# Weights cast by their transfers, attention inputs cast two tiles ahead, and first feed-forward groups of two tiles

## The chip, the core and the metric

The kernel runs on one core of a Trainium2 chip. The metric is the device time of one execution in microseconds (us). The engines are TensorE (PE; its weight loads are listed as PEld), VectorE (DVE), ScalarE (ACT), GpSimd (POOL) and SyncE (SP, which here only issues transfers). Each works through its own instructions in order and waits for the others by semaphores.

## What is computed

Block-wise linear attention with a decay per head, and then a feed-forward layer on the normalized result. Inputs and output are float32; batch 4, 8 heads, 768 positions, head width 64, model width 512, hidden width 2048.

```
# per head: lam; blocks of positions; state kv starts at 0 for each batch
intra = (q_b @ k_b.T) * (lam ** (i - j) for i >= j, else 0) @ v_b
inter = (q_b * lam ** (pos + 1)) @ kv
x     = intra + inter                                  # [batch, seq, 512]
kv    = lam ** block * kv + (k_b * lam ** (block - 1 - pos)).T @ v_b
xn    = (x - mean(x)) / sqrt(var(x) + 1e-6) * g_ln
out   = x + relu(xn @ w_ch1) @ w_ch2
```

## The kernel before

A tile is 128 positions of one batch with all heads and all 512 columns: 24 tiles, six per batch, t from 0 to 23, c = t mod 6 its place in the batch. Attention is done tile by tile with the block length 128. The decay of the mask is split: values are multiplied by lam to a negative power (lam_v), what comes out of the attention by lam to a positive power (lam_q), and the mask is a plain triangle (tril).

The work of a tile has five steps. p0 issues the loads of a later tile and casts q and k to bf16 and v times lam_v to bf16, all three on POOL (bf_inputs). p1 transposes k and q on PE (tk, tq) and copies them out of PSUM (kTp on ACT in two halves, qT on DVE). p2 computes the scores sc, masks them into mA on DVE, and, but for the last tile of a batch, the update pk of the state: for c = 0 Sn is written by DVE, otherwise DVE adds the old state (Stmp) and POOL multiplies by the block's decay (Sn). p3 computes po from mA and from the state of the tile before, scales it on DVE to x, and does the LayerNorm: stats, mv, xc (x minus its mean, bf16) on DVE, std on ACT, rstd on DVE. The scale g_ln is not in xc but multiplied into the rows of w_ch1; rstd comes last of all, in the output. p4 transposes xc (xt) and copies it to xT on ACT.

The feed-forward layer takes tiles in groups: [0..3], [4, 5], then four at a time, and the last [22, 23]. m1 is one of 16 units of a group, four matmuls with up to 512 columns into one PSUM buffer and a relu to hT on ACT. m2 is one of four parts of a tile, four matmuls; behind the last part DVE computes o = rstd times the sum, plus x, and SP stores it.

The order is written out by hand: nothing reorders it. The list `steps` holds the attention steps of tile after tile, shifted by one (p1 of tile j, p3 of j-1, p2 of j, p0 of j+1, p4 of j-1). The steps up to p4 of tile 3 run first. Then the steps of the next group's tiles are spread evenly between the units of a group. Weights come as float32 into six staging buffers by SP's queue and are cast by DVE, ACT and POOL in pieces between the units of the first group, w_ch1 times g_ln.

PSUM has two "aux" buffers, which tk, tq, pk and xt take in turn, so that of four allocations per round each waits for the reader of the last but one: a tk takes the buffer that pk had in the round before. There are three "mm" buffers for m1 and m2. k, q and v of a tile each have six input buffers.

Of the kernel before, what the change touches and what calls it, by code (L numbers as in the profile page):

```python
# [16 lines left out]
def kernel(  # L17
# [56 lines left out]
    def load_w1(c):  # L74
        f = wst.tile([128, KA, W1C], F32, tag="wst", name="w1f")
        nc.sync.dma_start(f, moe_w_ch1[:, c * W1C:(c + 1) * W1C].rearrange("(k p) f -> p k f", p=128))
        w_stage["w1", c] = f

    def load_w2(c):
        f = wst.tile([128, W2K, DM], F32, tag="wst", name="w2f")  # L80
        nc.sync.dma_start(f, moe_w_ch2[c * W2K * 128:(c + 1) * W2K * 128, :].rearrange("(k p) d -> p k d", p=128))
        w_stage["w2", c] = f

    def cast_w1(c):
        f = w_stage.pop(("w1", c))
        for kk in range(KA):
            dst = w1[:, kk, c * W1C:(c + 1) * W1C]
            if kk % 2 == 0:
                nc.vector.tensor_scalar_mul(dst, f[:, kk, :], g_col[:, kk:kk + 1])
            elif kk == 1:  # L90
                nc.scalar.mul(dst, f[:, kk, :], g_col[:, kk:kk + 1])
            else:
                nc.gpsimd.tensor_scalar_mul(dst, f[:, kk, :], g_col[:, kk:kk + 1])  # L93

    def cast_w2(c):
        f = w_stage.pop(("w2", c))
        for i in range(W2K):
            dst = w2[:, c * W2K + i, :]
            if i % 2 == 0:
                nc.vector.tensor_copy(dst, f[:, i, :])  # L100
            elif i == 1:
                nc.scalar.copy(dst, f[:, i, :])
            else:
                nc.gpsimd.tensor_copy(dst, f[:, i, :])
# [3 lines left out]
    load_tile(0)  # L108
    g_col = const.tile([128, KA], F32)
    nc.sync.dma_start(g_col, moe_g_ln.rearrange("(k p) -> p k", p=128))  # L110
    load_tile(1)
    load_tile(2)
    load_tile(3)
    load_w1(0)
    load_w1(1)
    load_tile(4)
    load_w1(2)
    load_w1(3)
    for c in range(NWC):
        load_w2(c)  # L120
    load_tile(5)
# [141 lines left out]
    def mlp_units(g):  # L263
        hT = gp.tile([128, KB, GT * 128], BF16, tag="hT", bufs=1, name="hT")
# [32 lines left out]
        for n in range(KB):  # L297
            yield "m1", n, lambda n=n: m1(n)

        lead = min(3, n_t) if g == 0 else 1  # L300
        order = [(i, part) for part in range(KB // 4) for i in range(lead)]
        order += [(i, part) for i in range(lead, n_t) for part in range(KB // 4)]
        for i, part in order:
            yield "m2", part, lambda i=i, part=part: m2(i, part)
# [13 lines left out]
    steps = [(p0, 0)]
    for j in range(NT + 1):
        lone = j - 1 == groups[0][-1]  # L320
        if j < NT and not lone:
# [71 lines left out]
```

## Time and profile before

| | |
|---|---|
| median of 3 runs | 271.66 us (270.94 to 271.92) |
| the profiled execution's own time | 271.69 us |
| its span, first to last instruction | 270.0 us |
| PE busy | 221.7 us (82%) |
| PEld busy | 128.6 us (48%) |
| DVE busy | 132.7 us (49%) |
| ACT busy | 113.2 us (42%) |
| POOL busy | 82.8 us (31%) |
| moved by DMA | 33.83 MB, mean 125 GB/s |

All times in the rows are counted from the start of the span. Busy times are sums over instructions; a matmul's length has its way through the array in it, so that a lone one is longer than one in a row of many. In brackets or behind a bar stands how long the engine was idle ahead of an instruction, and what released it.

### The profile page before, as it was taken

The numbers are of one execution on the slowest core, as the hardware profiler recorded it, in microseconds if no ns is written. First come the engines' busy times: TensorE is split into PE (matmuls) and PEld (weight loads), VectorE is DVE, ScalarE is ACT, GpSimd is POOL, SyncE is SP. The second block draws the span as 40 slices with busy tenths as digits, with TensorE's granted clock in tenths as the row PEclk, the third lists the DMA queues.
The fourth block names the chain that finished last, engine by engine and source line by source line (L and its number), as shares of the span: only waits on it lengthen the run. The fifth ranks groups of instructions, "written<-read, shape, count | busy, mean of one in ns | idle before, by whom it ended". The sixth has DMA issues, their size and how long they took to land. (4 is left out here: it accounts for less than half of the span.)

```text
span 270.0 us, 4247 instructions
## 1 busy us (share of the span) xinstructions
PE 221.7 (82%) x1638; PEld 128.6 (48%) x1664; DVE 132.7 (49%) x261; ACT 113.2 (42%) x223; POOL 82.8 (31%) x105
## 2 busy tenths in 40 slices
PE   0445448977995766999989999999999899999994
PEld 0334323533554563455545544555555454544761
DVE  2474492728466633754556525664555370335101
ACT  0542225844315523267521575225663217620540
POOL 1414557286002345370052254700513531000000
PEclk9999999999999979999999999999999999999999
DMA  6999964999989650594080971162000211001202
GB/s 129 206 268 304 379 232 164 270 194 225 218 212 240 121 117 0 125 211 93 2 191 8 255 143 31 44 153 79 0 2 0 78 41 39 0 30 50 78 2 78
DMA packets 83395, 33.83 MB, mean 125 GB/s; under 512 B 76080, under 2 KB 76336, under 8 KB 83376
## 3 DMA queue, kind: packets, MB, share of 16 engines
q1 hardware_dynamic: 79216, 32.52, 50.7%
q10 hardware_dynamic: 4160, 1.05, 2.2%
q8 instruction: 13, 0.21, 0.4%
q14 instruction: 6, 0.05, 0.1%
HBM read 27.27 MB, written 6.29 MB: 124 GB/s over the span
## 5 line engine op out<-in xcount | busy, mean ns | idle before, releaser
L271 PE MATMUL pm<-xT,w 128*128 128x512 bf16 (+1 forms) x435 | 93.8, 356 | 2.8 <-POOL w L93 1.1
L282 PE MATMUL pm<-w,hT 128*128 128x512 bf16 x371 | 88.6, 379 | 2.3 <-DVE w L100 1.6
L273 ACT ACTIVATE hT<-pm 128x512 bf16<-128x512 f32 (+1 forms) x112 | 58.3, 534 | 26.1 <-PE pm L271 24.3
L221 POOL TENSOR_TENSOR Sn<-Stmp,lamC 128x512 bf16<-128x512 f32 x16 | 20.4, 1277 | 130.4 <-DVE Stmp L220 130.4
L271 PEld LDWEIGHTS <-w 128*128 128x128 bf16 x448 | 42.8, 100 | 36.4 <-issue 3.0
L282 PEld LDWEIGHTS <-hT 128*128 128x128 bf16 x384 | 35.9, 98 | 38.3 <-DVE w L100 2.1
L193 DVE COPY qT<-tq 128x512 bf16<-128x512 bf16 x24 | 10.2, 424 | 58.8 <-PE tq L191 58.8
L185 PE MATMUL tk<-ident,kb 128*128 128x128 bf16 x96 | 10.3, 235 | 30.0 <-POOL kb L176 30.0
L293 DVE SCALAR_TENSOR_TENSOR o<-pm,rstd,x 128x512 f32<-128x512 f32 (+1 forms) x25 | 17.9, 724 | 32.8 <-PE pm L282 32.8
L206 DVE TENSOR_TENSOR mA<-sc,tril 128x512 bf16<-128x512 f32 x48 | 30.6, 678 | 3.8 <-PE sc L204 3.8
L236 DVE TENSOR_TENSOR x<-po,lam_q 128x512 f32<-128x512 f32 x24 | 16.6, 692 | 28.4 <-PE po L233 26.8
L260 ACT COPY xT<-xt 128x512 bf16<-128x512 bf16 x24 | 14.0, 585 | 35.9 <-PE xt L259 35.9
L245 ACT ACTIVATE std<-mv,eps_t 128x1 f32<-128x1 f32 x24 | 7.1, 295 | 47.2 <-DVE mv L241 47.2
L178 POOL TENSOR_TENSOR vb<-vin,lam_v 128x512 bf16<-128x512 f32 x24 | 25.5, 1063 | 3.4 <-DMA vin<-in_v_dram 1.8
L187 ACT COPY kTp<-tk 64x512 bf16<-64x512 bf16 x24 | 13.8, 575 | 30.2 <-PE tk L185 30.1
L185 PEld LDWEIGHTS <-kb 128*128 128x128 bf16 x96 | 6.6, 103 | 37.7 <-POOL kb L176 35.8
L204 PE MATMUL sc<-qT,kTp 128*128 128x128 bf16 x192 | 17.0, 237 | 2.5 <-DVE qT L193 2.4
L204 PEld LDWEIGHTS <-kTp 128*128 128x128 bf16 x192 | 14.2, 107 | 7.5 <-ACT kTp L188 1.7
L239 DVE BATCH_NORM_STATS2 stats<-x 128x6 f32<-128x512 f32 x24 | 16.7, 695 | 0.8
L174 POOL CAST qb<-qin 128x512 bf16<-128x512 f32 x24 | 15.0, 625 | 6.2 <-DMA qin<-in_q_dram 6.2
L176 POOL CAST kb<-kin 128x512 bf16<-128x512 f32 x24 | 14.9, 620 | 0.0
L259 PE MATMUL xt<-ident,xc 128*128 128x128 bf16 x96 | 10.2, 234 | 5.2 <-DVE xc L243 5.1
(44 smaller groups left out, 156.9 us busy)
## 6 DMA issues: line engine op xcount, KB each, us to landing
qin<-in_q_dram SPq DMA_DIRECT2D x24, 256.0 KB, 4.7
vin<-in_v_dram SPq DMA_DIRECT2D x24, 256.0 KB, 5.0
out_dram<-o SPq DMA_DIRECT2D x23, 256.0 KB, 2.2
kin<-in_k_dram SPq DMA_DIRECT2D x20, 256.0 KB, 4.9
w1f<-in_moe_w_ch_dram SPq DMA_DIRECT2D x4, 1024.0 KB, 7.4
w2f<-in_moe_w_ch_dram SPq DMA_DIRECT2D x4, 1024.0 KB, 8.5
kin<-in_k_dram ACTq DMA_DIRECT2D x4, 256.0 KB, 7.1
out_dram<-o SPq DMA_DIRECT2D x2, 128.0 KB, 1.7
```

Source lines behind the costliest of these rows:

```text
L174: nc.gpsimd.tensor_copy(qb, qf)
L178: nc.gpsimd.tensor_tensor(vb, vf, lam_v[:, :, None].to_broadcast([128, H, D]), op=ALU.mult)
L185: nc.tensor.transpose(tk[:, p, :], s["kb"][:, 2 * p:2 * p + 2, :], ident)
L204: nc.tensor.matmul(sc[:, i, :], lhsT=s["kT"][:, h // 2, h % 2, :], rhs=s["qT"][:, h // 2, :], start=(i == 0), stop=(i == H // 2 - 1), skip ...
L206: nc.vector.tensor_tensor(mA[:, half * (H // 2):(half + 1) * (H // 2), :], sc, tril[:, None, :].to_broadcast([128, H // 2, 128]), op=ALU.mult)
L221: nc.gpsimd.tensor_tensor(Sn, tmp, lamC, op=ALU.mult)
L236: nc.vector.tensor_tensor(x.rearrange("p (h d) -> p h d", h=H), po, lam_q[:, :, None].to_broadcast([128, H, D]), op=ALU.mult)
L239: nc.vector.bn_stats(stats, x)
L271: nc.tensor.matmul(pm[:, 0:N], lhsT=w1[:, kk, n * 128:(n + 1) * 128], rhs=xT_of[g][:, kk, 0:N], start=(kk == 0), stop=(kk == KA - 1))
L273: nc.scalar.activation(hT[:, n, 0:N], pm[:, 0:N], ACT.Relu)
L282: nc.tensor.matmul(acc[i], lhsT=hT[:, kk, i * 128:(i + 1) * 128], rhs=w2[:, kk, :], start=(kk == 0), stop=(kk == KB - 1))
L293: nc.vector.scalar_tensor_tensor(o[:, sl], in0=a[:, sl], scalar=rstd, in1=x[:, sl], op0=ALU.mult, op1=ALU.add)
```

## The change

The weights are loaded by POOL's queue with a cast on the way, straight into four bf16 tiles for w_ch1 and four for w_ch2; staging buffers and cast instructions are gone. g_ln is spread over all partitions (g_row) by one transfer on ACT's queue and multiplied in xc, which becomes a scalar_tensor_tensor. lam_q is multiplied in the cast of q, so that x is a plain copy out of PSUM, now on ACT. bf_inputs casts k first. The loads of k, q, v all go by SP's queue, k first; two memsets of one column on POOL hold the loads of tiles 4 and 5 back until POOL has come to that place. kb and vb have four buffers, xT three, hT two. The groups are [0, 1], [2, 3], [4, 5] and the rest as before; p0 of tile j+2 stands in round j; the order up to tile 5 is written out.

```diff
@@ load_tile @@
-        for name, src in (("q", q), ("k", k), ("v", v)):
+        for name, src in (("k", k), ("q", q), ("v", v)):
             f = inp.tile([128, H, D], F32, tag=name + "in", name=name + "in")
-            eng = nc.scalar if name == "k" and t < 4 else nc.sync
-            eng.dma_start(f, src[b, :, c * C:(c + 1) * C, :].rearrange("h p d -> p h d"))
-            got.append(f)
+            if after_pool:
+
+                nc.gpsimd.memset(f[:, 0, 0:1], 0.0)
+                after_pool = False
+            nc.sync.dma_start(f, src[b, :, c * C:(c + 1) * C, :].rearrange("h p d -> p h d"))
+            got[name] = f
...
     def load_w1(c):
-        f = wst.tile([128, KA, W1C], F32, tag="wst", name="w1f")
-        nc.sync.dma_start(f, moe_w_ch1[:, c * W1C:(c + 1) * W1C].rearrange("(k p) f -> p k f", p=128))
-        w_stage["w1", c] = f
+        nc.gpsimd.dma_start(w1[c], moe_w_ch1[:, c * W1C:(c + 1) * W1C].rearrange("(k p) f -> p k f", p=128))
...
-    g_col = const.tile([128, KA], F32)
-    nc.sync.dma_start(g_col, moe_g_ln.rearrange("(k p) -> p k", p=128))
...
+    g_row = const.tile([128, DM], F32)
+    nc.scalar.dma_start(g_row, moe_g_ln[None, :].to_broadcast([128, DM]))
...
+        kb = wk.tile([128, H, D], BF16, tag="kb", bufs=4, name="kb")
+        nc.gpsimd.tensor_copy(kb, f["k"])
         qb = wk.tile([128, H, D], BF16, tag="qb", name="qb")
-        nc.gpsimd.tensor_copy(qb, qf)
...
+        nc.gpsimd.tensor_tensor(qb, f["q"], lam_q[:, :, None].to_broadcast([128, H, D]), op=ALU.mult)
...
-        nc.vector.tensor_tensor(x.rearrange("p (h d) -> p h d", h=H), po,
-                                lam_q[:, :, None].to_broadcast([128, H, D]), op=ALU.mult)
+        nc.scalar.copy(x, po.rearrange("p h d -> p (h d)"))
...
-        nc.vector.tensor_scalar(xc, x, mv[:, 0:1], None, op0=ALU.subtract)
+        nc.vector.scalar_tensor_tensor(xc, in0=x, scalar=mv[:, 0:1], in1=g_row, op0=ALU.subtract, op1=ALU.mult)
...
-    groups = [[0, 1, 2, 3], [4, 5]]
+    groups = [[0, 1], [2, 3], [4, 5]]
...
+    def round_of(j):
+        steps = []
+        if j < NT:
+            steps.append((p1, j))
+        if j > 0:
+            steps.append((p3, j - 1))
+        if 0 < j and j + 2 < NT:
+            steps.append((p0, j + 2))
+        if j < NT:
+            steps.append((p2, j))
+        if j > 0:
+            steps.append((p4, j - 1))
+        return steps
...
+    p0(0)
+    p0(1)
+    run((p1, 0), (p2, 0))
+    bf_inputs(2)
+    load_w1(0)
+    load_w1(1)
+    run((p1, 1), (p3, 0), (p2, 1), (p4, 0))
+    bf_inputs(3)
+    load_w1(2)
+    load_w1(3)
+    run((p1, 2), (p3, 1), (p2, 2), (p4, 1))
+    load_tile(4, after_pool=True)
+    run((p1, 3), (p3, 2), (p2, 3))
+    for c in range(NWC):
+        load_w2(c)
+    load_tile(5, after_pool=True)
+    load_tile(6)
+    load_tile(7)
+    m1a, m2a = mlp(0)
+    m1b, m2b = mlp(1)
...
+    m1s(m1a, 0)
+    run((p4, 2), (p3, 3))
+    m1s(m1a, 1)
+    p4(3)
+    m1s(m1a, 2)
+    p0(4)
+    for c in range(3):
+        m1s(m1b, c)
+    m1s(m1a, 3)
+    p1(4)
+    m1s(m1b, 3)
+    order = [(m2a, i, part) for part in range(KB // 4) for i in range(2)]
+    order += [(m2b, i, part) for i in range(2) for part in range(KB // 4)]
+    extra = {0: [(p2, 4)], 2: [(p0, 5)], 3: [(p3, 4)], 6: [(p4, 4)], 7: [(p1, 5)], 8: [(p0, 6)], 10: [(p2, 5)], 12: [(p3, 5)], 13: [(p0, 7)], 15: [(p4, 5)]}
```

Three pieces show how instructions move. The first is POOL's order in the head of the kernel before, from the v cast of tile 1 to the state of tile 2.

```order
L178 TENSOR_TENSOR vb<-vin,lam_v 128x512
L221 TENSOR_TENSOR Sn<-Stmp,lamC 128x512
L174 CAST qb<-qin 128x512
L176 CAST kb<-kin 128x512
L178 TENSOR_TENSOR vb<-vin,lam_v 128x512
L221 TENSOR_TENSOR Sn<-Stmp,lamC 128x512
```

The casts of tile 2 stand behind the state of tile 1. Now the same place after the change, from the v cast of tile 2 on; w_0 to w_3 are the four tiles of w_ch1, kin is the input buffer of tile 4.

```order
L142 TENSOR_TENSOR vb<-vin,lam_v 128x512
L75 DMA w_0_75<-in_moe_w_ch_dram 128x4x512
L75 DMA w_1_76<-in_moe_w_ch_dram 128x4x512
L185 TENSOR_TENSOR Sn<-Stmp,lamC 128x512
L138 CAST kb<-kin 128x512
L140 TENSOR_TENSOR qb<-qin,lam_q 128x512
L142 TENSOR_TENSOR vb<-vin,lam_v 128x512
L75 DMA w_2_77<-in_moe_w_ch_dram 128x4x512
L75 DMA w_3_78<-in_moe_w_ch_dram 128x4x512
L185 TENSOR_TENSOR Sn<-Stmp,lamC 128x512
L63 MEMSET kin 128x1
L185 TENSOR_TENSOR Sn<-Stmp,lamC 128x512
```

The casts of tile 2 stand ahead of the state of tile 1, those of tile 3 ahead of the state of tile 2, and four weight transfers stand between them. The last pair is one round on DVE, first before the change.

```order
L193 COPY qT<-tq 128x512
L236 TENSOR_TENSOR x<-po,lam_q 128x512
L239 BN_STATS stats<-x 128x6
L241 BN_AGGR mv<-stats 128x2
L243 TENSOR_SCALAR xc<-x,mv 128x512
L247 RECIPROCAL rstd<-std 128x1
L206 TENSOR_TENSOR mA<-sc,tril 128x512 x2
L220 TENSOR_TENSOR Stmp<-pk,Sn 128x512
```

And after it:

```order
L157 COPY qT<-tq 128x512
L202 BN_STATS stats<-x 128x6
L204 BN_AGGR mv<-stats 128x2
L206 SCALAR_TENSOR_TENSOR xc<-x,mv,g_row 128x512
L210 RECIPROCAL rstd<-std 128x1
L170 TENSOR_TENSOR mA<-sc,tril 128x512 x2
L184 TENSOR_TENSOR Stmp<-pk,Sn 128x512
```

x has left the engine and xc has a second input; the LayerNorm of the tile before still stands ahead of the mask and of Stmp.

## Rows read from the trace of the kernel before

**Rows 1.** Busy us (and instructions) of each engine by stretch; then PEclk, DMA share, GB/s.

```profile
0.00:41.20 41.20, 16.23 (x141) 12.49 (x141) 22.18 (x47) 13.20 (x24) 16.57 (x26) 1.00 0.99 249
41.20:79.50 38.30, 33.99 (x211) 17.12 (x215) 20.55 (x38) 18.21 (x34) 16.85 (x20) 1.00 1.01 217
79.50:112.60 33.10, 23.62 (x236) 17.24 (x237) 18.76 (x38) 12.89 (x32) 10.37 (x13) 0.95 0.54 117
112.60:252.10 139.50, 133.94 (x960) 72.59 (x978) 68.78 (x135) 62.75 (x118) 39.00 (x48) 1.00 0.32 76
```

**Rows 2.** Timeline, tile 2's round: start, length, engine, line, operation [idle before, releaser].

```profile
22.53 0.61 PE L185 MATMUL tk<-ident,kb 128*128 128x128 bf16 x4 [3.70 <-POOL kb L176]
...
23.61 0.42 DVE L193 COPY qT<-tq 128x512 bf16<-128x512 bf16 x1 [3.58 <-PE tq L191]
...
23.84 0.58 ACT L188 COPY kTp<-tk 64x512 bf16<-64x512 bf16 x1
...
24.46 0.69 DVE L236 TENSOR_TENSOR x<-po,lam_q 128x512 f32<-128x512 f32 x1 [0.43 <-PE po L233]
...
25.20 0.64 PE L213 MATMUL pk<-vb,kb 128*128 128x128 bf16 x4
...
26.13 0.49 DVE L243 TENSOR_SCALAR xc<-x,mv 128x512 bf16<-128x512 f32 x1
...
27.79 0.68 DVE L220 TENSOR_TENSOR Stmp<-pk,Sn 128x512 f32<-128x512 f32 x1
...
28.55 1.26 POOL L221 TENSOR_TENSOR Sn<-Stmp,lamC 128x512 bf16<-128x512 f32 x1 [5.07 <-DVE Stmp L220]
...
30.31 0.61 POOL L176 CAST kb<-kin 128x512 bf16<-128x512 f32 x1
...
30.98 0.61 PE L185 MATMUL tk<-ident,kb 128*128 128x128 bf16 x4 [3.70 <-POOL kb L176]
```

**Rows 3.** PE's waits from 112.6 us to its end: total us, times, longest.

```profile
PE tk L185 <- POOL kb L176: 4.6, 7, 1.2
```

**Rows 4.** Timeline of the start: POOL and SP's queue.

```profile
2.31 2.85 SPq L110 DMA_DIRECT2D g_col<-in_moe_g_ln_dram  x1
...
6.93 0.61 POOL L174 CAST qb<-qin 128x512 bf16<-128x512 f32 x1 [4.98 <-DMA qin<-in_q_dram]
...
9.58 1.04 POOL L178 TENSOR_TENSOR vb<-vin,lam_v 128x512 bf16<-128x512 f32 x1 [1.48 <-ACT lam_v L155]
...
15.10 1.72 SPq L76 DMA_DIRECT2D w1f<-in_moe_w_ch_dram  x2
```

**Rows 5.** Groups by form: total busy us, mean ns, idle before them and releasers.

```profile
L273 ACT ACTIVATE hT<-pm 128x512 bf16<-128x512 f32 x80 | 46.6, 594 | 21.9 <-PE pm L271 20.9 <-PE pk L213 0.3
...
L178 POOL TENSOR_TENSOR vb<-vin,lam_v 128x512 bf16<-128x512 f32 x24 | 25.5, 1063 | 3.4 <-DMA vin<-in_v_dram 1.8 <-ACT lam_v L155 1.5
...
L293 DVE SCALAR_TENSOR_TENSOR o<-pm,rstd,x 128x512 f32<-128x512 f32 x23 | 17.0, 745 | 30.1 <-PE pm L282 30.1
...
L273 ACT ACTIVATE hT<-pm 128x256 bf16<-128x256 f32 x32 | 11.7, 383 | 4.2 <-PE pm L271 3.5
```

**Rows 6.** Chain that ended last, three of its PE pieces: start, length, piece.

```profile
216.90 0.45 PE sc L204 x8
...
217.57 2.59 PE pm L282 x12
...
252.10 7.12 PE pm L271 x64
```

**Rows 7.** Timeline, PE, the first long run of m1 matmuls.

```profile
41.76 5.96 PE L271 MATMUL pm<-xT,w 128*128 128x512 bf16 x18 [0.44 <-DVE w L89]
```

**Rows 8.** The page's GB/s of 40 equal slices of 6.75 us.

```profile
GB/s 129 206 268 304 379 232 164 270 194 225 218 212 240 121 117 0 125 211 93 2 191 8 255 143 31 44 153 79 0 2 0 78 41 39 0 30 50 78 2 78
```

**Rows 9.** The page's DMA issues: KB each, median us from issue to landing.

```profile
w1f<-in_moe_w_ch_dram SPq DMA_DIRECT2D x4, 1024.0 KB, 7.4
```

**Rows 10.** Timeline, DVE, the xc of tile 4.

```profile
60.72 0.97 DVE L243 TENSOR_SCALAR xc<-x,mv 128x512 bf16<-128x512 f32 x1
```

More of the change, by code (lines that the diff above doesn't have):

```diff
@@ L39 @@
     GT = 4
-    NG = NT // GT
     NWC = 4
@@ L74, in load_w1 @@
     def load_w1(c):
[L75 to L77 removed]
+        nc.gpsimd.dma_start(w1[c], moe_w_ch1[:, c * W1C:(c + 1) * W1C].rearrange("(k p) f -> p k f", p=128))
     def load_w2(c):
[L80 to L104, printed above, removed]
+        nc.gpsimd.dma_start(w2[c], moe_w_ch2[c * W2K * 128:(c + 1) * W2K * 128, :].rearrange("(k p) d -> p k d", p=128))
     lam_b = const.tile([128, H], F32)
     nc.sync.dma_start(lam_b, lam[None, :].to_broadcast([128, H]))
[L108 to L121 removed]
+    for t in range(4):
+        load_tile(t)
+    g_row = const.tile([128, DM], F32)
+    nc.scalar.dma_start(g_row, moe_g_ln[None, :].to_broadcast([128, DM]))
     ident = const.tile([128, 128], BF16)
@@ L295, in m2 @@
                     nc.sync.dma_start(out[b, c * C:(c + 1) * C, sl], o[:, sl])
[L297 to L304, printed above, removed]
-    groups = [[0, 1, 2, 3], [4, 5]]
+        return m1, m2
+    groups = [[0, 1], [2, 3], [4, 5]]
     while groups[-1][-1] < NT - 1:
@@ L312, in p0 @@
     def p0(t):
-        if t + 5 < NT and t > 0:
-            load_tile(t + 5)
+        if t > 3 and t + 4 < NT:
+            load_tile(t + 4)
         bf_inputs(t)
[L318 to L321, printed above, removed]
+    def round_of(j):
+        steps = []
+        if j < NT:
             steps.append((p1, j))
@@ L324, with run, m1s @@
             steps.append((p3, j - 1))
-        if j < NT and not lone:
+        if 0 < j and j + 2 < NT:
+            steps.append((p0, j + 2))
+        if j < NT:
             steps.append((p2, j))
-            if j + 1 < NT and j != groups[0][-1]:
-                steps.append((p0, j + 1))
         if j > 0:
             steps.append((p4, j - 1))
-        if lone:
-            steps += [(p0, j), (p1, j), (p2, j), (p0, j + 1)]
+        return steps
+    def run(*steps):
+        for f, *a in steps:
+            f(*a)
+    p0(0)
[18 more added lines that the diff above has]
+    m1b, m2b = mlp(1)
+    def m1s(f, c):
+        for n in range(c * W2K, (c + 1) * W2K):
+            f(n)
+    m1s(m1a, 0)
[12 more added lines that the diff above has]
+    extra = {0: [(p2, 4)], 2: [(p0, 5)], 3: [(p3, 4)], 6: [(p4, 4)], 7: [(p1, 5)], 8: [(p0, 6)], 10: [(p2, 5)], 12: [(p3, 5)], 13: [(p0, 7)], 15: [(p4, 5)]}
+    for u, (f, *a) in enumerate(order):
+        f(*a)
+        run(*extra.get(u, []))
+    steps = []
+    for j in range(6, NT + 1):
+        steps += [s for s in round_of(j) if s not in ((p3, 5), (p4, 5))]
     def upto(g):
@@ L337 @@
     pos = 0
-    def run_steps(end):
-        nonlocal pos
-        while pos < end:
-            f, t = steps[pos]
-            f(t)
-            pos += 1
-    run_steps(upto(0))
-    cast_w1(0)
-    w1_cast, w2_cast = 1, 0
-    for g in range(len(groups)):
-        units = list(mlp_units(g))
+    for g in range(2, len(groups)):
+        m1, m2 = mlp(g)
+        units = [(m1, n) for n in range(KB)]
+        units += [(m2, i, part) for i in range(len(groups[g])) for part in range(KB // 4)]
         first, end = pos, upto(g + 1)
         span = len(units) - 2
-        for u, (kind, n, unit) in enumerate(units):
-            if g == 0:
-                if kind == "m1" and n % 4 == 2 and w1_cast < NWC:
-                    cast_w1(w1_cast)
-                    w1_cast += 1
-                if (kind == "m1" and n == KB - 1) or (kind == "m2" and w2_cast < NWC and n >= w2_cast - 1):
-                    cast_w2(w2_cast)
-                    w2_cast += 1
-            unit()
-            run_steps(min(end, first + ((end - first) * (u + 1)) // span))
+        for u, (f, *a) in enumerate(units):
+            f(*a)
+            stop = min(end, first + ((end - first) * (u + 1)) // span)
+            run(*steps[pos:stop])
+            pos = stop
 _INS = ['q', 'k', 'v', 'lam', 'moe_g_ln', 'moe_w_ch1', 'moe_w_ch2']
```

28 lines of the change are left out of this document (12 added, 16 removed).

## The prediction

> **What bounds the kernel now.** I read the table of stretches first [rows 1]. Its columns show that TensorE (PE) is busy 16.2 of the first 41.2 us, 34.0 of the next 38.3 (the feed-forward part of tiles 0 to 3), 23.6 of the 33.1 after that (tiles 4 and 5), and 133.9 of 139.5 from 112.6 us on. So the late part is at its limit and all that can be won in bulk lies ahead of 112.6 us. What limits the head is in the timeline of one round, tile 2 [rows 2]: the first transposes tk start at 22.53, the last DVE instruction of the round, Stmp, ends at 28.47 (5.94 us later), POOL then needs Sn (1.26), qb and kb, and the next tk starts at 30.98. It waited 3.70 us for kb. The loop of 8.45 us per tile is therefore tk, copies, LayerNorm and mask on DVE, then three POOL instructions. From 112.6 us on the same wait for kb is still there seven times, 4.6 us in all [rows 3].
>
> The sum is made against the profiled execution: span 270.0, its time 271.69, so 1.7 lie around the span; the median of the runs is 271.66, the same to 0.03.
>
> **Part by part.** *Casts two tiles ahead.* kb(j) no longer stands behind Sn(j-1). What is late next is a PSUM buffer: tk, tq, pk and xt share two "aux" buffers, so tk(j+1) takes the one of pk(j) and waits until Stmp(j) has read it. The round becomes tk to Stmp: 5.94 us plus the edits on that path. x moves from DVE to ACT; there it follows the second kTp copy, which ends at 24.42, where DVE started it at 24.46 [rows 2]. A PSUM copy there costs 0.58 to 0.60 (the kTp row, the 512-wide hT row [rows 2, 5]) against 0.69, so -0.1. xc becomes a scalar_tensor_tensor, which takes 0.745 as o against 0.49 [rows 2, 5]: +0.25. Round: 6.1 us in place of 8.45. qb rises from a cast to a multiplication with a broadcast, 1.06 like vb [rows 5]; POOL then has about 0.6 + 1.06 + 1.06 + 1.26 = 4.0 us per tile, under 6.1, and no one waits for it as long as it runs ahead. Sn(j) is wanted only by Stmp(j+1) and by po in the round after.
>
> *The start.* g_col with its 2.85 us on SP's queue goes, g_row takes one 256 KB transfer on ACT's queue, and the four k loads leave that queue, behind which ACT made its tables: vb waited for lam_v until 9.58 [rows 4]. k is now the first load; q landed at 6.93 before. I put kb(0) at 5, qb(0) (needs lam_q, too) and vb(0) done at 8.8, Sn(0) at 11.4, Stmp(1) at 16.9 (tq(1) waits for pk(0)'s buffer, then about 5.5), Stmp(2) at 23.0. The first m1 matmul stands behind pk(3) in PE's order; pk ends 3.3 us into a round [rows 2]: 26.4 us, against 41.2. **Term A: -14.8.**
>
> *Weights by casting transfers on POOL's queue.* The 32 weight casts on DVE, ACT and POOL go. Two prices are not in the trace. How long POOL is held per transfer: SP needed 0.86 each for the same pieces, and 2.85 for g_col's 512 single values [rows 4]; I take 1.2, near the first. POOL issues w1_0 and w1_1 after vb(2), at 14.6, before Sn(1). At up to 2.5 us each nothing waits (Sn(1) done by 20.9, wanted by Stmp(2) near 22.4). At 2.85 each the delays pass through Sn(1), vb(3), Sn(2) and Sn(3) and cost about 4. How fast they land: a w1f piece took 7.4 us with another in flight [rows 9], the kernel moved 304 and 379 GB/s where weights dominated and 129 to 206 in the first two slices [rows 8]. At 304: w1_0 lands by 23, before 26.4. w2 is issued after Sn(3), about 31, with tiles 5 to 7 beside it, 6.5 MB in 21.5 us: the last chunk at 52.5 against a need near 51.5. I take +1. At 206 GB/s from 15.6 on the 8.4 MB take 41 us (+5), at 379 nothing waits.
>
> *The first two groups.* PE has 14.2 us of m1 (2 x 7.12), 64 x 0.216 = 13.8 of m2, and attention: a tile is 0.45 for the eight matmuls of sc, so 0.22 for the four each of tk, tq, pk and xt, and about 0.45 for po, 1.78; here tiles 4 and 5 and three remaining pieces, 4.2 [rows 6]. Sum 32.3. The first matmuls of the old stretch ran 18 in 5.96 us where 18 x 0.216 = 3.9 [rows 7]; I keep that loss of 2. ACT's 256-wide hT takes 0.383 of the 0.445 of a unit [rows 5, 6]; the 3.2 us of other copies in that stretch find only 2.0 of room: +1.2. With +1 for w2, 36.5: the stretch ends at 62.9. Before it took 38.3. **Term B: -1.8.**
>
> *The stretch of tiles 4 and 5.* Its matmuls are 14.0 plus attention of four and a half tiles, 8.3, so 22.3; but m1 units of 0.44 are too short to cover rounds of 6.1. 0.4 to the first tk, 4.0 for tile 6 (no state, no LayerNorm ahead of its mask, only the wait of tq(7) for pk(6)), three rounds of 6.1, and 6.1 us of matmuls behind tk(10): 28.8 against 33.1. **Term C: -4.3.**
>
> *From there on* work and order of PE are the same; its rounds of 8.7 us cover 6.1, so the 4.6 us of waits go [rows 3]. Bounds: 0 to -4.6. **Term D: -4.6.**
>
> *xc against POOL.* The old xc was seen at 0.97 where POOL was at work, against 0.49 [rows 2, 10]. xc now reads two tensors from SBUF while POOL's casts run at any time. Between nothing and one vb (1.06) in each of the seven rounds that bound (three in A, four in C), 0 to 7.4; I take **+3**, nearer to the first since POOL works 4.0 of 6.1 us and only part of an instruction is left when met. The Trainium skill ("SBUF — State Buffer", "Summary: rules for kernel authors") says that a VectorE instruction with two SBUF inputs and a GpSimd one that reads SBUF fully block each other, the second to issue waiting. By that rule in the worst phase the sum is 4.4 higher; the 0.97 agrees with the blocking, and does not tell how often it strikes.
>
> Span: 270.0 - 14.8 - 1.8 - 4.3 - 4.6 + 3 = 247.5; with 1.7 around it **249 us**, -8%.
>
> **Rivals.** *Weights come late.* Casting may move less than plain loads do; every us by which the last w2 chunk passes 51.5 is lost, since m2 of the first group needs it and what follows is at its limit. For: nothing in the trace casts on the way; the first slices show 129 and 206 GB/s. Against: pieces of 2 KB moved at 304 and more [rows 8]. At 206: 255; at 165, 51 us, the last chunk at 67: 264. The Trainium skill ("DMA: Bandwidth & Descriptors", section Bandwidth) has 6.15 us for 1 MB issued from GpSimd, without a cast; eight end to end would land at about 65, by which the sum is 262. No row here shows such a transfer.
>
> *Slower than before.* The same mechanism, further: the gain of 22.7 is used up when the last chunk lands at 51.5 + 22.7 = 74, that is below 8.4 MB / 58 us = 144 GB/s. At the slowest rate of the page, 129, it lands at 81: 278 us. For: that slice exists, with 256-byte pieces. Against: the weights' own slices are more than twice as fast.
>
> *POOL held by issuing.* Above 2.5 us each, at 2.85 to 4, 253 to 262. For: POOL writes them beside its casts; against: 0.86 on SP.
>
> *The round stays long.* If casts, not Stmp, still release tk (loads late, POOL behind), rounds stay at 8.45: A loses 4.7, C its 4.3, D its 4.6: 263.
>
> *The gain of D is larger or the chain shorter* (ACT frees x sooner, no xc collision): 244 to 246.
>
> **Chances.** Forecast with the small variations around it (243 to 255) 0.60, weights late 0.15, POOL held 0.09, long round 0.08, slower 0.07, something that cancels to no change 0.01. The range takes in late weights and a long round up to 265: 243 to 265. No change means within 0.5%, 1.4 us, about what this kernel's measurement can tell: faster 0.91, same 0.02, slower 0.07.
>
> **What would show it.** First m1 matmul near 26 us (A), with tk waiting for DVE's Stmp, not for POOL, and head rounds near 6.1. A w2 wait of about 1 us at m2 near 50 (B); more than 5 is the first rival. Two-tile stretch of tiles 4 and 5 near 29 us with tk waits of 1 to 2 us (C). No tk wait on kb after it (D). POOL's gap at its four w1 issues: under 2.5 each. xc's mean between 0.75 and 1.0. The forecast is wrong if m1 starts later than 32 us, if PE waits for a weight chunk more than 5 us in all, or if rounds are 8 us again.

## The result, and the profile after

The changed kernel takes **246.41 us** (246.32 to 246.46, four runs) where the kernel before took 271.79 in the same session (270.94 to 272.61): ratio 0.9066, 95% interval 0.9038 to 0.9094. The forecast was 249. The profiled execution has a span of 244.7 us and took 246.38, so 1.7 lie around the span, as before. Of the span, 25.3 us went (270.0 - 244.7).

The table of stretches of the changed kernel answers to [rows 1], cut at the places that correspond: the first m1, the start of the stretch of tiles 4 and 5, its end, and the place 17.9 us ahead of the end of the span (252.1 before). Columns: stretch, its length, busy us (and instructions) of PE, PEld, DVE, ACT, POOL, then granted clock, DMA share, GB/s.

```profile
0.00:27.50 27.50, 13.13 (x120) 11.20 (x121) 13.42 (x30) 12.79 (x22) 17.84 (x28) 1.00 1.07 183
27.50:62.90 35.40, 33.42 (x283) 23.18 (x281) 15.06 (x29) 18.41 (x47) 19.37 (x22) 1.00 1.13 204
62.90:93.10 30.20, 23.83 (x257) 17.42 (x257) 21.25 (x38) 16.82 (x39) 14.37 (x17) 1.00 1.09 226
93.10:226.80 133.70, 133.70 (x980) 73.23 (x979) 63.67 (x122) 68.69 (x132) 40.47 (x42) 1.00 0.32 75
226.80:244.70 17.90, 13.92 (x96) 9.06 (x93) 2.31 (x4) 6.13 (x16) 0.00 (x0) 0.96 0.12 44
```

| stretch | before, us | after, us | difference | forecast |
|---|---|---|---|---|
| head, to the first m1 (A) | 41.2 | 27.5 | -13.7 | -14.8 |
| feed-forward of tiles 0 to 3 (B) | 38.3 | 35.4 | -2.9 | -1.8 |
| tiles 4 and 5 (C) | 33.1 | 30.2 | -2.9 | -4.3 |
| the rest (D) | 157.4 | 151.6 | -5.8 | -4.6 |
| xc against POOL | | in A to C | | +3 |
| span | 270.0 | 244.7 | -25.3 | -22.5 |

Before, the first matmul of m1 starts at 40.74, 0.46 us ahead of the cut at 41.2; counted from it, A is -13.2 and B -3.4.

Read the fourth line of the fence: PE is busy for all of its 133.70 us. Before, the same work had 133.94 busy in 139.50 [rows 1]. By this measure the late part has reached its limit, and PE's waits lie in the first three stretches. The table of PE's waits of the changed kernel (for what, total us, times, longest) shows which:

```profile
PE tk L149 <- POOL kb L138: 6.7, 1, 6.7
PE xt L222 <- DVE xc L206: 4.9, 8, 1.2
PE tq L155 <- ACT kTp L152: 2.6, 2, 1.3
PE tk L149 <- ACT xT L223: 1.8, 4, 0.7
...
PE tq L155 <- DVE Stmp L184: 1.2, 3, 0.4
PE pm L234 <- DVE o L256: 1.1, 1, 1.1
```

The one wait of tk for kb is the very first transpose of the kernel, which waits for its input; the waits for POOL in the rounds and behind 112.6 us [rows 2, 3] are gone. No wait for a weight stands in the table. What holds the rounds now is LayerNorm (xc) and ACT's copies (kTp, xT).

The timeline of the changed kernel answers to [rows 2]: tile 2's round, from tk to the next tk.

```profile
17.38 0.59 PE L149 MATMUL tk<-ident,kb 128*128 128x128 bf16 x4 [0.67 <-ACT xT L223]
...
18.66 0.58 ACT L152 COPY kTp<-tk 64x512 bf16<-64x512 bf16 x1
...
19.30 0.59 PE L155 MATMUL tq<-ident,qb 128*128 128x128 bf16 x4 [1.33 <-ACT kTp L152]
...
20.77 0.58 ACT L200 COPY x<-po 128x512 f32<-128x512 f32 x1 [1.53 <-PE po L197]
...
22.34 0.75 DVE L206 SCALAR_TENSOR_TENSOR xc<-x,mv,g_row 128x512 bf16<-128x512 f32 x1
...
24.26 0.68 DVE L184 TENSOR_TENSOR Stmp<-pk,Sn 128x512 f32<-128x512 f32 x1
24.43 0.59 PE L149 MATMUL tk<-ident,kb 128*128 128x128 bf16 x4 [0.67 <-ACT xT L223]
```

tk starts again after 7.05 us (8.45 before). It was let go by ACT's copy xT, not by Stmp: at 24.43 Stmp has only begun. And tq waits 1.33 us until both kTp copies of its own tile have read tk: tq has to take tk's buffer.

The transfers of the weights. First POOL's issues in the timeline, then the page's lines for their landing (median, by bytes written) and their queue, beside [rows 4, 9]:

```profile
16.89 1.68 POOL L75 DMA_DIRECT2D w<-in_moe_w_ch_dram  x2
...
22.35 1.55 POOL L75 DMA_DIRECT2D w<-in_moe_w_ch_dram  x2
...
31.93 3.03 POOL L78 DMA_DIRECT2D w<-in_moe_w_ch_dram  x4
```

```profile
q0 software_dynamic: 4224, 4.19, 10.8%
...
w<-in_moe_w_ch_dram POOLq DMA_DIRECT2D x8, 512.0 KB, 7.8
```

POOL is held 0.76 to 0.84 us by each (the mean of a row), as SP was. The queue's packets take 10.8% of 16 engines over the span, 26.4 us of all engines, for 8.39 MB read in fp32 (4.19 are written in bf16): 318 GB/s of source. That is an estimate, since packet times overlap (the DMA share above goes to 1.13); it is a rate like the 304 and 379 of the old fp32 loads [rows 8].

### The profile page after: what moved, and what is told of

The parts are those of the page before. It is cut to its first block, busy times and chain, and to the rows that moved or that the text cites. A ratio compares the mean times of both kernels' runs of the same rounds, so it can differ in the third digit from the quotient of the medians.

```text
span 244.7 us, 4375 instructions
## 1 busy us (share of the span) xinstructions
PE 218.0 (89%) x1728; PEld 134.1 (55%) x1728; DVE 115.7 (47%) x221; ACT 122.8 (50%) x255; POOL 92.0 (38%) x107
## 3 DMA queue, kind: packets, MB, share of 16 engines
q0 software_dynamic: 4224, 4.19, 10.8%
## 4 chain that ended last, share of the span: by engine, by line
PE 67%; SPq 11%; DVE 9%; DMA 4%; ACT 3%; POOL 2%; issue 2%; DVEq 0%; ACTq 0%; POOLq 0%
PE pm L245 26%; PE pm L234 26%; SPq L65 11%; PE sc L168 3%; PE tq L155 3%; DVE mA L170 2%; DMA qin<-in_q_dram 2%; PE po L193 2%; DVE stats L202 2%; PE xt L222 2%; DVE xc L206 2%; PE tk L149 2%; PE po L197 2%; ACT x L200 2%; DMA out_dram<-o 2%
## 5 line engine op out<-in xcount | busy, mean ns | idle before, releaser
L234 PE MATMUL pm<-xT,w 128*128 128x256 bf16 (+1 forms) x512 | 92.1, 327 | 2.9 <-ACT hT L236 1.2
L245 PE MATMUL pm<-w,hT 128*128 128x512 bf16 x384 | 90.2, 379 | 0.0
L236 ACT ACTIVATE hT<-pm 128x512 bf16<-128x512 f32 (+1 forms) x128 | 59.5, 488 | 23.1 <-PE pm L234 20.5
L234 PEld LDWEIGHTS <-w 128*128 128x128 bf16 x512 | 48.5, 98 | 30.7 <-issue 3.6
L140 POOL TENSOR_TENSOR qb<-qin,lam_q 128x512 bf16<-128x512 f32 x24 | 25.1, 1044 | 9.1 <-issue 4.8
L142 POOL TENSOR_TENSOR vb<-vin,lam_v 128x512 bf16<-128x512 f32 x24 | 26.2, 1093 | 2.1 <-PE po L193 1.7
L200 ACT COPY x<-po 128x512 f32<-128x512 f32 x24 | 14.0, 584 | 19.6 <-PE po L197 18.4
L206 DVE SCALAR_TENSOR_TENSOR xc<-x,mv,g_row 128x512 bf16<-128x512 f32 x24 | 21.8, 909 | 0.9
L138 POOL CAST kb<-kin 128x512 bf16<-128x512 f32 x24 | 15.6, 651 | 5.5 <-DMA kin<-in_k_dram 5.2
L155 PE MATMUL tq<-ident,qb 128*128 128x128 bf16 x96 | 10.1, 233 | 5.7 <-ACT kTp L152 2.6
```

The source lines that it names most:

```text
L140: nc.gpsimd.tensor_tensor(qb, f["q"], lam_q[:, :, None].to_broadcast([128, H, D]), op=ALU.mult)
L142: nc.gpsimd.tensor_tensor(vb, f["v"], lam_v[:, :, None].to_broadcast([128, H, D]), op=ALU.mult)
L200: nc.scalar.copy(x, po.rearrange("p h d -> p (h d)"))
L206: nc.vector.scalar_tensor_tensor(xc, in0=x, scalar=mv[:, 0:1], in1=g_row, op0=ALU.subtract, op1=ALU.mult)
L234: nc.tensor.matmul(pm[:, 0:N], lhsT=w1[n // W2K][:, kk, (n % W2K) * 128:(n % W2K + 1) * 128], rhs=xT_of[g][:, kk, 0:N], start=(kk == 0), s ...
L236: nc.scalar.activation(hT[:, n, 0:N], pm[:, 0:N], ACT.Relu)
```

## The experiments

Twelve kernels were run; the table leaves out the first form of one, told below. "After" is the changed kernel, "before" the other; ratios are against before, in the same session.

| kernel | us | ratio, 95% interval |
|---|---|---|
| before + casting transfers | 272.5 | 1.0005, 0.9969 to 1.0042 |
| before + look-ahead | 259.09 | 0.9528, 0.9492 to 0.9565 |
| after, casts behind the state | 269.4 | 0.9912, 0.9877 to 0.9947 |
| after, first group of four | 251.33 | 0.9248, 0.9208 to 0.9289 |
| after, decay at x | 245.79 | 0.9045, 0.9000 to 0.9090 |
| after | 246.41 | 0.9066, 0.9038 to 0.9094 |
| after, w2 loaded twice | 257.15 | 0.9465, 0.9441 to 0.9490 |
| after, no hold-back | 245.96 | 0.9057, 0.9035 to 0.9079 |
| after, six buffers of o | 245.64 | 0.9053, 0.9018 to 0.9088 |
| after, LayerNorm from PSUM | 244.53 | 0.9000, 0.8962 to 0.9038 |
| the same, copy of x behind xc | 248.68 | 0.9157, 0.9135 to 0.9180 |
| the same, copy behind xT, six o | **239.15** | 0.8801, 0.8769 to 0.8832 |

### Which part brings the gain

**Casts behind the state again.** Everything of the change stays, but a tile's casts stand behind Sn.

```diff
-        if 0 < j and j + 2 < NT:
-            steps.append((p0, j + 2))
         if j < NT:
             steps.append((p2, j))
+        if 0 < j and j + 1 < NT:
+            steps.append((p0, j + 1))
...
-    bf_inputs(2)
...
-    run((p1, 1), (p3, 0), (p2, 1), (p4, 0))
-    bf_inputs(3)
+    run((p1, 1), (p3, 0), (p2, 1), (bf_inputs, 2), (p4, 0))
...
```

> The changed kernel with one part undone: the casts of the next tile stand behind the state Sn of this one again (p0 of j+1 behind p2 of j), as in the kernel before. Theory (the loop through POOL set the round): rounds of 8.3 us in place of 6.3 in the stretch of tiles 4 and 5 (3 of them, +6), 8.4 in place of 7.05 in the head (2 of them, +2.7), and the waits for kb after it back (+3 to 4.6): 258 us (255 to 260), with PE's tk waiting for kb. Rival (the early start and the weights are the whole gain, the round is bound by DVE either way): 246 to 248.

269.4 us: 23 of the 25 us are lost. The direction of the theory holds, its size doesn't. Its table of waits shows both why and what was forgotten:

```profile
PE tk L149 <- POOL kb L138: 23.0, 10, 6.9
PE tq L155 <- POOL qb L140: 7.9, 13, 1.0
```

qb, now a multiplication of 1.04 us behind kb, makes tq wait as well. Tile 2's round is 8.63 us (tk at 20.00 and 28.63), m1 starts at 32.17, the stretch of tiles 4 and 5 takes 38.15 against 29.77 from first m1 to first m1, and the rest 161.2 against 151.6. So the rest of the change, without the look-ahead and with qb's multiplication in the round's way, has small worth: 2.3 us below before.

**Casting transfers alone**, the opposite cut: before, with the weights as in after and g_ln in xc, the order untouched.

```diff
-    f = wst.tile([128, KA, W1C], F32, tag="wst", name="w1f")
-    nc.sync.dma_start(f, moe_w_ch1[...])
+    nc.gpsimd.dma_start(w1[c], moe_w_ch1[...])
...
-    cast_w1(0)
```

> The kernel before with one part of the change alone: weights by casting transfers on POOL's queue, g_ln in xc; groups, order of the steps and x on DVE as before. Theory (the casts cost about 1 us ahead of the first m1 and some 5 us of PE's waits inside the first group, the round stays long): 265 (262 to 268). Rival (the casting transfers are most of the gain): 255 or less. If casting transfers or their issue hurt: 272 or more.

273.77 us (272.39 to 275.73; ratio 1.0087, 1.0049 to 1.0125), 8 us above the theory and inside the third case, that the transfers hurt. Part of it was my own edit: g_row stood behind the k loads on ACT's queue and held up the tables of decays (vb(0) waited 3.88 us for lam_v, the first m1 came at 44.39). So it was run again with g_row on the inputs' queue:

> As the run of the kernel before with casting transfers, but g_row is loaded on the inputs' queue behind tile 3, so that the table of decays isn't delayed behind it, which cost about 3 us at the start there (273.77). Theory: the casting transfers alone are worth only the waits of the second stretch on casts, and the round of the head, which POOL's casts hold, stays: 268 to 271 us, first m1 at 41 to 42. Rival: without the 3 us the casts' removal shows in full: 265 or less.

272.5 us (270.3 to 274.31), no difference from before, in the sense of the theory and a little past its range. Its waits for casts of weights are gone, but the one that counts is not, in its table of PE's waits:

```profile
PE tk L151 <- POOL kb L142: 31.1, 13, 8.0
```

The same table of the kernel before has, over the whole span:

```profile
PE tk L185 <- POOL kb L176: 30.0, 14, 8.1
...
PE tq L191 <- ACT kTp L188: 1.3, 1, 1.3
```

So the wait is as long as it was (the second line is used further down). Taking 32 casts off three engines gives nothing while the round waits for POOL.

**The look-ahead alone**: before, with kb and vb in four buffers and each tile's casts ahead of the state update.

```diff
-        kb = wk.tile([128, H, D], BF16, tag="kb", name="kb")
+        kb = wk.tile([128, H, D], BF16, tag="kb", bufs=4, name="kb")
...
+        if 0 < j and j + 2 < NT and j + 2 not in (4, 5, 6):
+            steps.append((p0, j + 2))
         if j < NT and not lone:
             steps.append((p2, j))
-            if j + 1 < NT and j != groups[0][-1]:
-                steps.append((p0, j + 1))
...
```

> The kernel before with one thing changed: the casts of a tile stand two tiles ahead, before the state update on POOL (four buffers for kb and vb). Weights still come as fp32 and are cast by the engines, the groups are as before, decay and g_ln as before. Theory (the casts behind the state are what held the round, and the run that put them back lost 23 of 25 us): much of the gain comes by this alone, in the head (first m1 near 35 instead of 41.2) and behind 112.6 (the 12.8 us of waits for kb go, and some of the slow clock); but the casts of the weights, ready no earlier, take back part of the head: 256 us (250 to 262). Rival: the weights' casts in fp32 fill what POOL and DVE gain and the head is bound by their landing: 263 to 270. If the look-ahead were all, it would be 249.

259.09 us: -12.8 by itself against the kernel before of its session (271.86), within the theory's range. (Behind 112.6 us of the kernel before the waits for kb are 4.6 us [rows 3], not the 12.8 of the expectation.) The first m1 comes at 36.32, and now the weights are late in the old way: two lines of its table of waits are the casts of weights by POOL and DVE.

```profile
PE pm L271 <- POOL w L93: 5.7, 1, 5.7
...
PE pm L282 <- DVE w L100: 2.4, 1, 2.4
```

These waits are 8.1 us, and the next kernel, which has the casting transfers as well, has none of them.

**First group of four tiles**, everything else as in after.

```diff
-    groups = [[0, 1], [2, 3], [4, 5]]
+    groups = [[0, 1, 2, 3], [4, 5]]
```

> The changed kernel with its first group of four tiles again (512 columns per m1 matmul, m1 only behind p4 of tile 3). Theory (two-tile groups start PE on m1 while tiles 2 and 3 are finished): m1 starts near 33 us in place of 27.5, about 1 us is won back since ACT's hT no longer limits m1: 251 (249 to 253). Rival (PE's work is the same and the hole only moves): 246 to 247.

251.33 us, as expected: the small groups are worth 4.9 us; the first m1 comes at 34.61. This kernel has the look-ahead together with the casting transfers and is 7.8 us under the look-ahead alone, so the casting transfers, worth nothing on the old round, may be worth something on the short one. The 7.8 us are not theirs alone, though: this kernel also loads its inputs in another order and by other queues (first tk at 6.72 us, 8.20 in the look-ahead alone), and its waits for xc are 8.3 us against 5.4. How the 7.8 divide was not run.

**The decay back at x.**

```diff
-        nc.gpsimd.tensor_tensor(qb, f["q"], lam_q[...], op=ALU.mult)
+        nc.gpsimd.tensor_copy(qb, f["q"])
...
-        nc.scalar.copy(x, po)
+        nc.vector.tensor_tensor(x, po, lam_q[...], op=ALU.mult)
```

> The kernel after with one part undone: the query's decay is multiplied into x again, on DVE (692 ns in the kernel before), and qb is a plain copy on POOL (625 ns where the multiplication takes 1.04 us). Theory: with the casts two tiles ahead POOL has room, so the 0.4 us per tile that POOL is spared off the path is worth nothing by itself; x on DVE takes 0.69 in place of ACT's 0.58 but spares the hop to ACT, and DVE gets 24 x 0.69 = 17 us more work of which none is on the path after the third stretch: 246 to 247 us. Rival: vb starts 0.4 us earlier on POOL and gets clear of the centring, which loses its 0.77 us of blocking per round: 243.5 to 245.5. Other side: DVE, with x in its queue, delays qT, Stmp and mA, rounds of 6.6 or more: 248 to 250.

245.79 us (245.48 to 246.05), just under the theory's range and above the rival's. Its interval overlaps that of after, so a difference of 0.6 is not shown; this part of the change brought no gain that the runs can tell. The timeline of the third stretch in this kernel shows half of what the rival named:

```profile
76.72 1.04 POOL L142 TENSOR_TENSOR vb<-vin,lam_v 128x512 bf16<-128x512 f32 x1
77.34 0.97 DVE L207 SCALAR_TENSOR_TENSOR xc<-x,mv,g_row 128x512 bf16<-128x512 f32 x1
```

vb starts 0.62 us ahead of xc instead of 0.07, so xc takes 0.97 and not 1.53, and the rounds 5.87 and 5.89 (73.57, 79.44, 85.33) against 6.32 and 6.34. What that wins is in part lost ahead of them: the one m1 that waits for o waits 2.1 us here, 1.1 in after.

### How far the rivals of late weights were away

**Each w2 chunk twice**, the first copy into a spare tile that nothing reads.

```diff
     for c in range(NWC):
+        w2x = const.tile([128, W2K, DM], BF16, name=f"w2x_{c}")
+        nc.gpsimd.dma_start(w2x, moe_w_ch2[...])
         load_w2(c)
```

> Each of the four w2 chunks is loaded twice, the first time into a spare tile that nothing reads: 4.19 MB more to read over the same queue. By the 26.4 us of engine time that the casting queue takes for 8.39 MB, the doubled part costs 13.2 us more of the transfers. Theory (the margin of the last w2 chunk is about 2 us): the last chunk lands 13 us later, near 62, against a need at 51: about 10 us of waits of the second product on w2, 254 to 259 us. Rival: room beside the loads of the tiles hides most of it: under 250. The run measures how far the forecast's rival of late weights was away.

257.15 us, 10.7 more than after, as the theory has it. In the timeline of its PE:

```profile
54.52 3.57 PE L245 MATMUL pm<-w,hT 128*128 128x512 bf16 x8 [4.37 <-DMA w<-in_moe_w_ch_dram]
61.28 1.44 PE L245 MATMUL pm<-w,hT 128*128 128x512 bf16 x3 [3.19 <-DMA w<-in_moe_w_ch_dram]
```

The waits for w2 are 7.8 us in all; with them PE's clock fell (granted 0.50; eight matmuls that take 1.89 at full clock took 3.57), and that is about the other 3 us. By the 26.4 us above, the doubled part is 13.2 us of transfers; 7.8 of waits leave a margin of about 5 us, an estimate. So the rival of late weights was a real one, and what kept it off is the measured rate of the casting queue.

**No hold-back of the inputs of tiles 4 and 5.**

```diff
-    for t in range(4):
+    for t in range(6):
         load_tile(t)
...
-    load_tile(4, after_pool=True)
...
-    load_tile(5, after_pool=True)
```

> The inputs of tiles 4 and 5 are loaded right behind those of tile 3 instead of being held back until POOL has issued the weight transfers. That is 1.57 MB more ahead of the weights. At the 183 to 204 GB/s of the first two stretches these take 7.7 to 8.6 us of transfer time. Theory: the transfers are the limit until w1 has landed, so the first m1, which now waits for nothing, waits for w1: 248 to 254 us, first m1 at 29 to 35. Rival: the sixteen engines have room in the head, the weights land as before or within their margin of 2 us: 245.5 to 247.

245.96 us: the rival is right, the theory wrong. 1.57 MB ahead of the weights cost nothing, first m1 at 27.69; the first stretch moved 200 GB/s instead of 183. The transfers were not at a limit that the rates of two stretches show.

### What holds the rounds now

**Six buffers for o.** Near 65 us an m1 waited 1.08 us for a store, in the third buffer of o.

```diff
-                o = wk.tile([128, DM], F32, tag="o", name="o")
+                o = wk.tile([128, DM], F32, tag="o", bufs=6, name="o")
```

> The output tile o gets six buffers instead of three. After the change the seventh row of the profile's waits shows an m1 that waits 1.08 us near 65.9, because the DVE that frees its accumulator waited 2.8 us for an out_dram transfer that still held a buffer of o. Theory: that wait is on the path and goes: 245.3 us (244.5 to 246.0). Rival: the PE work behind it absorbs it and something else ends there (pm on hT): 246.2 to 246.7, no change.

245.64 us (245.23 to 246.85): the wait for o is gone from PE's table, and the median moves by 0.8 as the theory says, but the runs overlap those of after; by time alone it isn't told. The profiled execution has a loss of its own: the granted clock was 0.50 from 80 to 82 us, and that round took 7.46 us (tk at 78.45 and 85.91) where after has 6.34.

**LayerNorm from PSUM.** The statistics and xc read po, not x.

```diff
-        nc.vector.bn_stats(stats, x)
+        nc.vector.bn_stats(stats, po)
...
-        nc.vector.scalar_tensor_tensor(xc, in0=x, ...)
+        nc.vector.scalar_tensor_tensor(xc, in0=po, ...)
```

> The changed kernel with stats and xc read from po in PSUM in place of ACT's copy x; x is still copied for the output. Theory (in the rounds that bound, tk to tk, lie the wait for x on ACT, 1.1 us, and xc's 0.78 us behind POOL's vb because both read from SBUF): rounds of 6.3 us become about 5.0 in the stretch of tiles 4 and 5 and 7.05 becomes 6.4 in the head, -4 to -5: 242 (240 to 243.5), xc at 0.75 throughout. Rival (another wait, kTp or xT on ACT, ends last just behind it): 245 to 247.

244.53 us, between the two. One round from the timeline of the third stretch, in after:

```profile
73.23 0.38 PE L149 MATMUL tk<-ident,kb 128*128 128x128 bf16 x4 [0.24 <-ACT xT L223]
...
76.82 1.04 POOL L142 TENSOR_TENSOR vb<-vin,lam_v 128x512 bf16<-128x512 f32 x1
...
76.89 1.53 DVE L206 SCALAR_TENSOR_TENSOR xc<-x,mv,g_row 128x512 bf16<-128x512 f32 x1
...
79.55 0.38 PE L149 MATMUL tk<-ident,kb 128*128 128x128 bf16 x4 [0.24 <-ACT xT L223]
```

and the same in this kernel, with its statistics:

```profile
73.41 0.38 PE L149 MATMUL tk<-ident,kb 128*128 128x128 bf16 x4 [0.24 <-ACT xT L223]
...
76.11 0.70 DVE L202 BATCH_NORM_STATS2 stats<-po 128x6 f32<-128x512 f32 x1 [1.09 <-ACT x L200]
...
76.99 1.04 POOL L142 TENSOR_TENSOR vb<-vin,lam_v 128x512 bf16<-128x512 f32 x1
77.06 0.75 DVE L206 SCALAR_TENSOR_TENSOR xc<-po,mv,g_row 128x512 bf16<-128x512 f32 x1
...
78.94 0.38 PE L149 MATMUL tk<-ident,kb 128*128 128x128 bf16 x4 [0.24 <-ACT xT L223]
```

xc starts 0.07 us behind vb in both; with one of its two big operands in PSUM it isn't held up. Its mean over the kernel falls from 909 to 751 ns, and this round from 6.32 to 5.53 us, the 0.78 of the blocking; the next falls from 6.34 to 5.81. But the statistics still wait for ACT's copy, though they no longer need x: the copy reads po first in the program, and the second reader is let go behind it. Hence the next run.

**The copy of x behind xc**, otherwise the same.

```diff
-        nc.scalar.copy(x, po.rearrange("p h d -> p (h d)"))
         stats = wk.tile([128, 6], F32, tag="stats", name="stats")
...
         nc.vector.scalar_tensor_tensor(xc, ...)
+        nc.scalar.copy(x, po.rearrange("p h d -> p (h d)"))
```

> As the run with the layernorm read from PSUM (244.53), and ACT's copy of the attention output into x is emitted behind the centring, so that the statistics start as soon as the matmuls of po end. Theory: the statistics waited 1.09 us for that copy in every round, and in the rounds of the third stretch (5.5 and 5.8 us) that wait was on the path: rounds of 4.8 to 5.2, the stretch 2 us shorter, the head 1 us shorter: 242.0 us (240.5 to 243.5). Rival: the chain then ends on the casts of POOL or on Stmp instead, and nothing is gained: 244 to 245. Other side: po has one buffer, and x, copied last, holds it 0.7 us longer, which delays the next tile's po: over 245.

248.68 us, slower by 4 than with the copy ahead. The time fits the third case (over 245), but not for its reason: the table of waits has no wait of po for x. In its timeline the statistics start right behind po, but:

```profile
79.22 0.75 DVE L205 SCALAR_TENSOR_TENSOR xc<-po,mv,g_row 128x512 bf16<-128x512 f32 x1
80.06 0.59 ACT L206 COPY x<-po 128x512 f32<-128x512 f32 x1 [1.72 <-DVE xc L205]
81.53 0.61 ACT L223 COPY xT<-xt 128x512 bf16<-128x512 bf16 x1
82.19 0.38 PE L149 MATMUL tk<-ident,kb 128*128 128x128 bf16 x4 [0.43 <-ACT xT L223]
```

The copy waits for xc and then, with the square root, stands on ACT ahead of xT, for which tk waits (3.7 us in all, 1.8 with the copy ahead). PE's waits for ACT's other products rise with it: for hT from 1.3 to 3.8, for kTp from 2.6 to 3.9, while those for xc fall from 2.5 to 0.8. The wait was moved, not removed.

**The copy behind xT**, with root and reciprocal, and six buffers for o.

```diff
         nc.scalar.copy(xT_of[g][...], xt)
+        po, x, mv = s["rest"]
+        nc.scalar.copy(x, po)
+        nc.scalar.activation(std, mv[:, 1:2], ACT.Sqrt, bias=eps_t)
+        nc.vector.reciprocal(rstd, std)
```

> The last run moved the wait: with the copy of x behind the centring, ACT made it just ahead of xT, and the next tile's tk then waited for xT (3.7 us in all). Here the statistics and the centring read po, the copy of x, the square root and the reciprocal come behind the copy of xT, and o has six buffers. Theory: round = tk, kTp, po, stats, xc, xt, xT, all without the copy of x: 5.0 to 5.4 us in the third stretch instead of 5.8 to 6.3, and 0.8 for o: 242.0 us (240.5 to 243.5). Rival: po, held until the copy behind xT, delays the matmuls of the next tile's po, or another wait (tq on Stmp, pm on hT) takes over: 243.5 to 246, where the run with the copy ahead stood at 244.53.

**239.15 us** (238.76 to 239.86), faster than both kernels and than the theory. The rows of its third stretch:

```profile
68.79 0.38 PE L149 MATMUL tk<-ident,kb 128*128 128x128 bf16 x4 [0.29 <-ACT xT L218]
...
70.76 0.70 DVE L201 BATCH_NORM_STATS2 stats<-po 128x6 f32<-128x512 f32 x1 [0.47 <-PE po L197]
...
71.71 0.75 DVE L205 SCALAR_TENSOR_TENSOR xc<-po,mv,g_row 128x512 bf16<-128x512 f32 x1
...
73.02 0.58 ACT L218 COPY xT<-xt 128x512 bf16<-128x512 bf16 x1
73.49 0.60 ACT L220 COPY x<-po 128x512 f32<-128x512 f32 x1
...
73.65 0.38 PE L149 MATMUL tk<-ident,kb 128*128 128x128 bf16 x4 [0.29 <-ACT xT L218]
```

This round is 4.86 us; the three of the stretch are 5.24, 4.86 and 5.69 where after has 5.84, 6.32 and 6.34 (tk at 67.39, 73.23, 79.55, 85.89). The hold of po that the rival named shows once, 1.2 us. The span is 7.7 shorter than that of after: first m1 at 24.95 (-2.6), from there to the first m1 of tiles 4 and 5 35.34 (-0.4), that stretch 25.16 instead of 29.77 (-4.6), the rest the same to 0.1. How much of the 7.7 is o's alone was not run.

## Why the prediction was right, and where it was not

The mechanism is the predicted one: casts ahead of the state shorten the round, and the head, tiles 4 and 5 and the last part gain by it. By itself it brings 12.8 of the 25 us, and without it 2 are left. Term by term:

- **A (-14.8, measured -13.7).** kb(0) came at 6.07 instead of 5, Sn(0) ended at 12.05 instead of 11.4; tk(2) started at 17.38 where my sum has 16.9; tile 2's round adds 0.95 (7.05 instead of 6.1), and the last piece, from tk(3) to the first m1, gives 0.3 back.
- **The step that failed: "tk(j+1) takes the one of pk(j) and waits until Stmp(j) has read it"** (the section on the kernel before says the same of the buffers). By the waits it is another sharing of the two aux buffers: tk waits for ACT's xT, so it takes that of xt; tq waits for Stmp (0.4 at most), or in the rounds of tiles 1 and 2 for the kTp copies of its own tile (1.27 and 1.33), so there it takes tk's. The old kernel's table of waits has that wait once, 1.3 us (the line shown above), a row that I didn't use. In tile 2's round it covers most of the 0.95 us by which that is longer than predicted; that share is read from the chain and was not run. In C the size came out all the same: rounds of 5.84, 6.32 and 6.34 against 6.1, of which 0.78 in each of the last two is blocked xc; with LayerNorm from PSUM they are 5.53 and 5.81. The waits of tk there are 0.24 us, not the 1 to 2 that I named as a sign.
- **B (-1.8, measured -2.9).** Two charges did not fall due, or not in full: no wait for w2 (+1), and the first m1 matmuls were hardly slow (16 of 256 columns in 2.33 us, 1.91 in the run with the copy behind xT: 0.4 of the 2). ACT's hT made PE wait 1.2, as charged. What I had too small is PE's work: 33.4 us busy, those 0.4 among them, against a sum of 32.3.
- **C (-4.3, measured -2.9), and xc against POOL (+3).** Three of the four xc in C took 1.53, 1.53 and 1.09 instead of 0.75, 1.9 us in all; none of the three in the head was hit. +3 for seven rounds was thus somewhat too much, and what came due lies in C; two xc in B were hit as well (1.29 and 1.11), with PE's waits of 0.36 and 0.17 us behind them. What C lost besides is 1.1 us for a store that still held o, at 65.9, and 1.1 us from tk(10) to its end (7.17 where I had 6.1). Part of its gain is clock, which my sum left out: 0.95 granted there before [rows 1], 1.00 now. The blocking was hardly chance: POOL's casts follow Sn, Sn follows Stmp, and so vb meets xc in the same phase in two rounds running (vb 0.07 us ahead at 76.82, 0.06 at 83.14). The second to start waits for the first: xc ends 0.55 to 0.56 behind vb, whether it started 0.07 us behind it (after) or 0.62 (decay at x). The Trainium skill's rule ("SBUF — State Buffer", "Summary: rules for kernel authors"), that the second to issue waits, agrees with these rows. With one of the operands in PSUM xc takes 751 ns in the mean, and 0.75 us at the same phase.
- **D (-4.6, measured -5.8).** The seven waits for kb went, and so did the rest of the idle time: 139.50 - 133.94 = 5.56 us of it [rows 1] are now none.
- **The rivals.** POOL was held 0.8 per transfer where I took 1.2 and had 2.5 as the point from which it costs. The weights moved at an estimated 318 GB/s; the last was issued at 34.2 and the longest took 14.6 us to land, so all had landed by 49, where I had 52.5. The doubled w2 shows that 4.2 MB more costs 10.7 us, so the point was near. The long round fell with the first m1 at 27.5; put back, it gives 269.4, where I had 263: qb's wait (7.9) and the clock (0.79 granted from 82 to 90 us in that run) were left out there.

Terms A to D were off by +1.1, -1.1, +1.4 and -1.2, which cancel to +0.2 by luck; the +3 charged for xc came due as 1.9, and lies in C. So the span is 2.8 under the forecast, and the sum is better than its terms.

## What to carry to other kernels

Find the loop that carries the wait before counting work: 32 casts fewer were worth nothing while one queue's order held the round; once it didn't, the same edit together with the rest of the change brought 7.8 us. When a wait goes, find for every shared buffer who had it last, by the waits in a trace and not by the order of the program alone, since that reader may be what is late next. An instruction that nobody needs soon (here the copy of x) belongs behind the one that somebody waits for, on the same engine: that, with more buffers for o, made the difference between 248.7 and 239.2.

## What the hardware showed that was not expected

- Casting transfers from POOL's queue cost nothing visible against plain ones: 0.76 to 0.84 us of POOL for each 1 MB of source, a median of 7.8 us to landing (7.4 before [rows 9]), about 318 GB/s of source while they run (the estimate above).
- While PE waited 4.37 us for w2 in the run with doubled loads, the granted clock fell to 0.50 (1.2 of 2.4 GHz), and it stayed there through the second wait of 3.19 us to 65 us: waits of 7.8 us cost 10.7. In the kernel after the record has 1.00 through the first 226.8 us.
- In the head four small transposes take 0.59 to 0.61 us and the eight matmuls of sc 1.06; from the first m1 on it is 0.39 and 0.61, with a granted clock of 1.00 on record in both stretches. The run with the casts behind the state has the same slow lengths under a recorded 0.50: 0.61 (tq at 29.64) and 1.06 (sc at 30.89), then 0.39 (xt at 34.94) once the record is back at 1.00. So the head of both kernels has the lengths of the lower level, 1.2 GHz, and its recorded 1.00 does not fit them; why the record says so, the runs don't tell.
